# Moving the wait for the output weights from TensorE to SyncE, in a decode attention block

## Chip, cores and metric

One core of a Trainium2 chip. The metric is device time in microseconds (us) of one execution, as the median of several runs; lower is better. All runs that are compared are fast unless a run is called slow (here: over 1.5% above the fastest run of the same kernel). "Span" is the profiled time from the first to the last instruction, some 1.8 us shorter than the device time.

## The reference, cut to what matters

```python
B, Sq, D = (8, 1, 512);  Hq, Hkv, Sk, Dh = (32, 8, 8192, 128)          # bf16
mod = (_silu(c) @ w_mod).reshape(8, 6, 1, -1)                          # sa, ca, ga, sb, cb, gb
h = _layernorm(x) * (1 + ca) + sa
q = (h @ wq) ...                                                       # 32 heads, 4 to a key/value head
p = _softmax(einsum('bhqd,bhkd->bhqk', q, k) * Dh ** (-0.5))
x = x + ga * (einsum('bhqk,bhkd->bhqd', p, v) ... @ wo)                # wo: 4096 x 512
h = _layernorm(x) * (1 + cb) + sb
x = x + gb * (relu(h @ w1 + b1) ** 2 @ w2 + b2)                        # 512 -> 1792 -> 512
```

The key and value caches are 268 MB of the 284 MB that are read.

## The kernel before

Every engine has a list of operations with their dependencies; a dependency becomes a wait on a semaphore in front of the operation. TensorE, VectorE and ScalarE run a hardware loop over the 8 batches; SyncE issues all loads unrolled.

```python
# _looped: waits on what is loaded outside the loop are emitted in front of the loop
for i in range(passes):
    for p in "ab":
        for j, o in enumerate(self._part(e, (i, p))):
            want = self._want(e, o, i)
            ...
            self._emit(eng, None, {s: v for s, v in want.items() if s not in per}, seen)
with nc.Fori(0, passes, ...) as i:
    ...                                        # part "a": every pass
    with eng.If(i < passes - 1):               # part "b": every pass but the last
        ...
```

```python
RING = sb("ring", [128, NSLOT, UNIT], BF16)    # NSLOT = 4 slots of 4 MB: two heads' keys or values
units = [(kv, b, p) for b in range(B) for kv in "kv" for p in range(NP)]     # 4 key, 4 value loads a batch

def load(n):
    ...
    dep = [released.get(s)]                    # the last reader of slot n % 4
    ...                                        # (the last value load goes in four pieces)
    loaded[n] = dma("sync", s_ring[s], lambda e: e.dma_start(slot(s), src), dep)

load(0)
load(1)
...                                            # three small bias loads
d_wo = dma("sync", s_wo, ...)                  # output weights, 4 MB
load(2)
load(3)
```

```python
for b in range(B):
    for p in range(NP):                        # keys: transpose on TensorE (L488), copy out, scores (L505)
        for k in range(4):
            t, toks = key_tiles(n, k, qn % 2)
            ...
            if k == 3:
                released[n % NSLOT] = score_first[0]
                load(n + NSLOT)
    ...                                        # softmax
    for p in range(NP):                        # values (L636)
        if p == NP - 1:                        # projection of 24 of 32 heads, reads wo_sb (L543)
            proj_done = project(...)
            values(0, 16, 28)
        ...                                    # one of the four L660 matmuls releases the slot, then load(n + NSLOT)
# behind the loop: the last value load, the last projection (L731, reads wo_sb), the MLP
```

`pe_stream` and `pe_stream32` issue filler matmuls whose results nobody reads.

## Time and profile before

| | before |
|---|---|
| device time, median | 668.92 us (668.77 to 669.64, 3 runs) |
| span | 667.0 us |
| bytes read | 283.66 MB |
| DMA share of the span, SyncE's queue | 99.2% |
| TensorE busy; mean granted clock | 79%; 0.945 |
| TensorE idle before its first key transpose | 25.53 us, ended by the landing of `wo` |

The lines are in the prediction below. To read them: a group or timeline line is "start, duration, engine, source line, operation, output<-inputs, shapes, count", and the bracket behind it is the engine's idle time just before and what ended it. In the stretches, the last three columns are the granted TensorE clock, the busy share of the 16 DMA engines and GB/s.

### The profile page before, as it was taken

What the parts mean: (1) busy time and instruction counts of PE and PEld (TensorE: products, weight loads), DVE (VectorE), ACT (ScalarE), POOL (GpSimd) and SP (SyncE); (2) the same over time, 40 slices, a digit from 0 to 9 for tenths busy, and PEclk for the clock granted to TensorE, in tenths of its full rate; (3) what the DMA queues carried; (4) which work ended last, traced back from release to release, by engine and by line L of the source; (5) the groups of instructions that cost most, each with busy time, mean ns of one, the idle gap of its engine ahead of it and who ended that gap; (6) DMA issues with size and microseconds to landing.
All of it is one profiled execution on the core that took longest, in us unless ns stands there. A gap on an engine that the chain in (4) does not pass through costs nothing.

```text
span 667.0 us, 15923 instructions
## 1 busy us (share of the span) xinstructions
PE 523.9 (79%) x7259; PEld 349.1 (52%) x7259; DVE 307.6 (46%) x587; ACT 264.4 (40%) x307; POOL 20.6 (3%) x79
## 2 busy tenths in 40 slices
PE   3309988898849987699858988399875997589887
PEld 2207753675328742477327753287434773277535
DVE  1105662567216651367314663166523673156623
ACT  2105661466106651266314661156512663146611
POOL 7400000000000000000000000000000000000000
PEclk9999999999979999799987999799997999889996
DMA  9999999999999999999999999999999999999997
GB/s 374 439 409 437 431 417 437 432 426 432 438 428 426 434 440 428 424 436 436 428 426 438 428 430 432 438 428 424 436 438 430 424 436 430 430 432 436 428 418 278
DMA packets 12188, 283.85 MB, mean 426 GB/s; under 512 B 1260, under 2 KB 1296, under 8 KB 3600
## 3 DMA queue, kind: packets, MB, share of 16 engines
q1 hardware_dynamic: 12128, 283.65, 99.2%
q8 instruction: 9, 0.15, 0.1%
q10 hardware_dynamic: 48, 0.02, 0.0%
q14 instruction: 3, 0.02, 0.0%
HBM read 283.66 MB, written 0.01 MB: 425 GB/s over the span
## 4 chain that ended last, share of the span: by engine, by line
PE 54%; DMA 36%; ACT 6%; DVE 2%; issue 1%; POOL 0%; SPq 0%; POOLq 0%; DVEq 0%
PE PS L488 37%; DMA ring<-in_A_k_cache_dram 25%; PE PS L505 10%; DMA wo_sb<-in_A_wo_dram 7%; ACT P_sb L582 5%; DMA ring<-in_A_v_cache_dram 4%; PE PS L636 2%; PE PS L478 1%; ACT KTb L493 1%; DVE O_sb L656 1%; PE PS L472 1%; PE PS L594 1%; DVE Pm L608 0%; PE PS L614 0%; PE PS L773 0%
## 5 line engine op out<-in xcount | busy, mean ns | idle before, releaser
L488 PE MATMUL PS<-IDENT,ring 128*128 128x128 bf16 x4096 | 262.4, 225 | 63.1 <-DMA ring<-in_A_k_cache_dram 35.7
L488 PEld LDWEIGHTS PS<-IDENT,ring 128*128 128x128 bf16 x4096 | 241.9, 101 | 111.4 <-issue 48.1
L493 ACT ACTIVATE KTb<-PS 128x1024 bf16<-128x1024 bf16 x192 | 196.7, 1024 | 234.4 <-PE PS L488 234.4
L495 DVE COPY KTb<-PS 128x1024 bf16<-128x1024 bf16 x320 | 209.7, 687 | 149.1 <-PE PS L488 146.9
L636 PE MATMUL PS<-ring,Pm 128*32 128x512 bf16 x1018 | 66.5, 405 | 23.5 <-DMA ring<-in_A_v_cache_dram 22.7
L505 PE MATMUL PS<-KTb,Qb 128*32 128x512 bf16 x1024 | 78.8, 384 | 4.5 <-ACT KTb L493 4.5
L656 DVE CAST O_sb<-PS 128x512 bf16<-128x512 f32 x31 | 21.4, 692 | 110.3 <-PE PS L636 110.3
L636 PEld LDWEIGHTS PS<-ring,Pm 128*32 128x32 bf16 x1018 | 26.6, 101 | 60.2 <-DMA ring<-in_A_v_cache_dram 31.4
L535 ACT ACTIVATE KTb<-PS 32x192 bf16<-32x192 f32 (+1 forms) x18 | 5.6, 311 | 112.1 <-PE PS L472 105.6
L582 ACT ACTIVATE P_sb<-PS,negm 128x1024 bf16<-128x1024 f32 x32 | 35.2, 1113 | 20.2 <-DVE negm L577 20.2
L478 PE MATMUL PS<-ONES 128*128 128x512 f32 x80 | 42.1, 630 | 0.0
L472 PE MATMUL PS<-IDENT 128*128 128x512 bf16 x112 | 33.4, 380 | 0.0
L594 PE MATMUL PS<-IDENT,P_sb 128*128 128x128 bf16 x256 | 19.8, 220 | 15.4 <-ACT P_sb L582 15.4
L608 DVE COPY Pm<-PS 64x512 bf16<-64x512 bf16 x48 | 20.2, 421 | 25.1 <-PE PS L594 24.6
L594 PEld LDWEIGHTS PS<-IDENT,P_sb 128*128 128x128 bf16 x256 | 14.4, 98 | 25.2 <-ACT P_sb L582 25.2
L505 PEld LDWEIGHTS PS<-KTb,Qb 128*32 128x32 bf16 x1024 | 15.4, 94 | 21.0 <-ACT KTb L493 8.5
L512 DVE TENSOR_REDUCE m<-PS 128x1 f32<-128x512 f32 x32 | 22.0, 689 | 6.6 <-PE PS L505 6.6
L660 PEld LDWEIGHTS PS<-SEL,O_sb 128*128 128x128 bf16 x124 | 5.8, 97 | 29.4 <-DVE O_sb L656 29.4
L478 PEld LDWEIGHTS PS<-ONES 128*128 128x128 f32 x80 | 12.7, 190 | 10.6 <-issue 10.6
L660 PE MATMUL PS<-SEL,O_sb 128*128 128x8 bf16 x124 | 7.8, 169 | 12.3 <-DVE O_sb L656 12.0
L472 PEld LDWEIGHTS PS<-IDENT 128*128 128x128 bf16 x112 | 9.9, 104 | 10.1 <-issue 7.2
L543 PE MATMUL PS<-wo_sb,KTb 128*32 128x512 bf16 x192 | 11.8, 380 | 3.3 <-ACT KTb L535 3.3
(134 smaller groups left out, 150.1 us busy)
## 6 DMA issues: line engine op xcount, KB each, us to landing
ring<-in_A_k_cache_dram SPq DMA_DIRECT2D x32, 4096.0 KB, 32.1
ring<-in_A_v_cache_dram SPq DMA_DIRECT2D x31, 4096.0 KB, 27.9
ring<-in_A_wq_dram SPq DMA_DIRECT2D x1, 4096.0 KB, 20.1
wo_sb<-in_A_wo_dram SPq DMA_DIRECT2D x1, 4096.0 KB, 46.7
ring<-in_w_mod_dram SPq DMA_DIRECT2D x1, 3072.0 KB, 10.5
ring<-in_A_v_cache_dram SPq DMA_DIRECT2D x1, 2048.0 KB, 23.1
ring<-in_B_w_dram SPq DMA_DIRECT2D x3, 512.0 KB, 19.7
ring<-in_B_w_dram SPq DMA_DIRECT2D x1, 1344.0 KB, 18.5
```

The lines of the kernel that those rows point to most:

```text
L472: ts = [op("tensor", lambda e: e.matmul(bank(at).rearrange("p (a r) -> p a r", a=4), IDENT[:, :], rhs)) for _ in range(n)]
L478: ts = [op("tensor", lambda e: e.matmul(bank(at).rearrange("p (a r) -> p a r", a=4), ONES[:, :], rhs)) for _ in range(n)]
L488: t = op("tensor", lambda e, j=j, i=i: e.matmul(STG[j][:, i, :], src[:, 32 * k + 8 * j + i, :], IDENT[:, :], is_transpose=True), [loaded[n ...
L493: stg_free[j] = op("scalar", lambda e, j=j, dst=dst: e.activation(dst, STG[j], ACT.Copy), [t])
L495: stg_free[j] = op("vector", lambda e, j=j, dst=dst: e.tensor_copy(dst, STG[j]), [t])
L505: t = op("tensor", lambda e, hf=hf, q=q, rhs=rhs: e.matmul(PS[32 * q:32 * (q + 1), k, :], Qb[:, 2 * p + hf, :], rhs, start=(p == 0 and hf ...
L512: return op("vector", lambda e: e.tensor_reduce(m4[:, k:k + 1], bank(k), AX.X, ALU.max), [t])
L582: exps.append(op("scalar", lambda e, k=k: e.activation(P_sb[:, k, :, :, :], bank(k).rearrange("p (i x) -> p i x", i=8).unsqueeze(2).to_bro ...
L594: t = op("tensor", lambda e, k=k, i=i: e.matmul(STG[k][:, i, :], P_sb[:, k, i, :, :].rearrange("p h x -> p (h x)"), IDENT[:, :], is_transp ...
L608: done.append(op("vector", lambda e, dst=dst, frm=frm: e.tensor_copy(dst, frm), [t, k_pm]))
L636: t = op("tensor", lambda e, m=m, cg=cg, p=p, vt=vt, Obank=Obank: e.matmul(Obank[32 * cg:32 * (cg + 1), :], lhs[:, p, 32 * m:32 * m + 32], ...
L656: t = op("vector", lambda e, osb=osb, Obank=Obank: e.tensor_copy(osb, Obank), [t])
```

## The change

The intent: TensorE should not stand at the loop's entry for the output weights, which it first reads after the values of three pairs of heads. SyncE waits for them instead before it issues the fifth load; TensorE waits for that load before it comes to the projection, so the order still holds. The whole diff:

```diff
-            dep = [released.get(s)]
+            dep = [released.get(s), d_wo if n == NSLOT else None]
...
                         wo_sb[:, 4 * g + j, :], start=(g == 0), stop=(g == 5), tile_position=(0, 32 * j)),
-                        k_oP + [d_wo])
+                        k_oP)
```

## The prediction

> **What bounds the kernel now.** I read four views in this order: the page (engine shares, the 40 slices, the DMA queues), the chain that ended last, the timelines of TensorE and SyncE around the wait in question, and the DMA's share stretch by stretch. First the page:
>
> ```profile
> PE 523.9 (79%) x7259; PEld 349.1 (52%) x7259; DVE 307.6 (46%) x587; ACT 264.4 (40%) x307; POOL 20.6 (3%) x79
> ...
> DMA  9999999999999999999999999999999999999997
> GB/s 374 439 409 437 431 417 437 432 426 432 438 428 426 434 440 428 424 436 436 428 426 438 428 430 432 438 428 424 436 438 430 424 436 430 430 432 436 428 418 278
> ...
> q1 hardware_dynamic: 12128, 283.65, 99.2%
> ```
>
> The DMA row is at its top digit in every slice but the last. SyncE's queue q1 alone carries 283.65 MB and fills 99.2% of the time of all sixteen DMA engines. TensorE is busy 79% of the span, so it waits somewhere for a fifth of it. Now the chain of waits and the timeline of TensorE:
>
> ```profile
> 4.21 46.74 DMA wo_sb<-in_A_wo_dram
> 51.65 5.00 PE PS L488 x64
> ...
> 107.23 22.50 DMA ring<-in_A_k_cache_dram
> ```
>
> ```profile
> 25.82 0.29 PE L435 MATMUL PS<-KTb 128*128 128x32 bf16 x4 [0.48 <-ACT KTb L432]
> 51.65 5.00 PE L488 MATMUL PS<-IDENT,ring 128*128 128x128 bf16 x64 [25.53 <-DMA wo_sb<-in_A_wo_dram]
> ```
>
> The first fence (start, length, what) says that the chain runs through the 4 MB load of the output weights (`wo`) from 4.21 to 50.95 us, and then through TensorE's key transposes. The second says that TensorE does nothing for 25.53 us in front of its first key transpose and is released by that load. This is the visible prize. But the wait is not needed by the transposes: the program puts every wait of the loop on something loaded outside it in front of the loop, and the projection, which does read `wo`, starts only at 113.96 us.
>
> The question is whether TensorE's lost 25 us reach the end. The stretches (busy time of PE, PEld, DVE, ACT, POOL, then clock, DMA share, GB/s) say no:
>
> ```profile
> 27.50:51.50 24.00, 0.00 (x0) 0.00 (x0) 0.23 (x1) 0.00 (x0) 1.47 (x5) 1.00 1.00 418
> 51.50:120.00 68.50, 61.55 (x871) 41.41 (x871) 37.09 (x68) 32.19 (x37) 0.00 (x0) 1.00 1.01 431
> 120.00:640.00 520.00, 428.40 (x5956) 287.36 (x5960) 256.62 (x467) 223.38 (x256) 0.00 (x0) 0.94 1.00 432
> ```
>
> While TensorE stands still, the DMA engines are full (share 1.00, 418 GB/s), and in the two later stretches they are just as full. The idle time belongs to an engine that is not the bound.
>
> Landings confirm it. From the trace's completion records, the sixteenth completion of each 4 MB load comes at 30.92 us (key load 0), 40.66 (key 1), 50.94 (`wo`), 61.00 (key 2), 70.84 (key 3), 81.17, 90.88, 100.60, 110.31 (the four value loads) and 120.02 (the first key load of batch 1). From 120.02 on they come every 9.716 us: 54 loads later, at 644.69, (644.69 - 120.02)/54. This is 4.194 MB / 9.716 us = 432 GB/s without a pause. The end hangs on the same stream: the value chunks are all in at 654.67, and the last chunk of the second MLP weight at 663.56. The last MLP matmuls are stopped by it: the step between their starts is 0.15 us right after that landing against 0.03 us among the others. The span ends 3.4 us later, at 667.0.
>
> [...] `wo`, issued at 4.21, lands after 46.74 us just by standing behind earlier loads. [...] Key load 2's issue in the timeline of SyncE is such a one (14.98 to 37.63); the 24 us it blocks hurt nothing, because queued bytes cover them.
>
> ```profile
> 14.98 23.70 SPq L369 DMA_DIRECT2D ring<-in_A_k_cache_dram  x2
> 61.87 0.33 SPq L369 DMA_DIRECT2D ring<-in_A_v_cache_dram  x1
> ```
>
> **The change part by part.**
> 1. *TensorE's wait in front of the loop goes.* It then waits for key load 0, landed at 30.92. Between `wo`'s landing and the first transpose lay 51.65 - 50.94 = 0.7 us (loop entry); part of the entry can now be done earlier, so the first transpose comes at 31.0 to 31.6, 20 us sooner.
> 2. *TensorE in batch 0 then runs into the loads.* A key load costs it 9.76 us (four times 1.89 of transposes and 0.55 of scores), nearly the DMA's 9.7. Key 0 until 41, key 1 until 51, then it stands 10 us until key 2 lands at 61.00. Key 3 lands at 70.84, just as key 2 is done; key 3 is done by 80.6. Softmax took 10.5 us before (from 90.8 to the first value matmul at 101.33), so values start near 91; loads 2 and 3 of them land only at 100.60 and 110.31, and the last values are done near 113.5 instead of 118.2. The next key load lands at 120.02. TensorE started batch 1 at 120.08 before and will start it there again. All 20 us are given back inside batch 0: worth at the end 0.0.
> 3. *SyncE's wait comes in front of the fifth load (value 0).* Slot 0 comes free near 41.5, `wo` lands at 50.94: the issue moves from 61.87 to about 51.0. At 51.0 the queue still holds key 2 and 3, until 70.84, i.e. 19.8 us of work. Before, at 61.87, it held 70.84 - 61.87 = 9.0 us. So the margin grows, but it was never used up: cost 0.0, gain 0.0.
> 4. *Ordering.* TensorE needs `wo` only after value loads, which SyncE issues after its wait. So nothing is added in the loop. The projection of the last two heads (L731) lies behind the loop and keeps its wait; as TensorE no longer waits in front of the loop, the wait is now actually emitted: about 0.05 us (TensorE's waits show 51 ns in the trace) on the final chain, partly behind the last MLP weights. I count 0 to +0.1.
>
> Sum: -0.0 - 0.0 + 0.05, on 668.92.
>
> **The rivals.**
> *(a) TensorE's head start is kept*: 51.65 - 31.5 = 20 us off, 648.8, 3.0% faster. For it: the chain, which charges 7.0% to the `wo` load, and TensorE's 79%. Against it: no DMA pause anywhere into which the loads could move forward; [...] after batch 0 TensorE waits again (the 22.50 us piece above is the stream, seen from TensorE).
> *(b) The stream is a little looser early on, and deeper queueing tightens it.* Slices 3 and 6 show 409 and 417 GB/s, and between `wo` and value 0 the spread from the first to the last engine's completion grows from 1.2 to 2.3 us and stays. If an earlier issue cured that, about -1.1 us, 667.8. Against it: the engine completing first keeps its 9.7 us step throughout, and the growth falls together with 16 KB instruction fetches (nine in the trace, near 1.1 us each, seven of them from 55 to 111). These have to come anyway, only sooner.
> *(c) SyncE's wait starves the queue.* It would take `wo` landing later than 70.8; slowed by early fetches it might land a microsecond later, not 20. If it did occur, some us slower, 670 to 675.
> *(d) SyncE's issue becomes slow because more is queued.* Issues later in this trace with 25.9 us of work ahead take the same 0.33 us. 0.0.
>
> **Range and chances.** The three runs before lie from 668.77 to 669.64. I take 668.8, with -1.0 for (b) and +1.0 for the spread of runs and point 4. Two percent is 13.4 us: only (a) comes near on the one side and a starved queue on the other, and both contradict the DMA row, so 2% for faster and 1% for slower.
>
> **What would show it.** In the changed profile: the first key transpose near 31.5 us; the value 0 issue near 51 and value 1 right behind it; a wait of SyncE on `wo` of about 12 us; a TensorE gap of some 10 us before key load 2 and others among the values; the first key transpose of batch 1 at 120 us as before; landings and the last MLP weight's landing within 1 us of before; DMA share 99%. The prediction is wrong if TensorE's batch 1 starts well before 120, if any slice shows DMA under 9, or if the steady step between landings differs from 9.72 us.

"Such a one", in front of SyncE's timeline, means an issue that takes long; the one named took 22.6 us (14.98 to 37.63), with the DMA share at 0.98 and 421 GB/s meanwhile. 0.0, 0.0 and 0.05 on 668.92 come to 668.97, and I took 668.8, in 667.8 to 669.8. For loads already issued, the trace of the changed kernel shows: while SyncE waited (38.60 to 51.31 us), they went on at a DMA share of 1.01 and 408 GB/s.

## The result, and the profile after

| | before | after |
|---|---|---|
| device time, median | 668.85 us (668.68 to 669.64, 4 runs) | 668.37 us (668.15 to 668.45, 4 runs) |
| ratio, 95% interval | | 0.999 (0.9973 to 1.0007) |
| span | 667.0 us | 666.7 us |
| first key transpose | 51.65 us | 30.84 us |
| value load 0 issued | 61.87 us | 51.38 us |
| first key transpose of batch 1 | 120.08 us | 119.86 us |
| last MLP weight landed | 663.56 us | 663.33 us |
| mean granted TensorE clock | 0.945 | 0.918 |

A ratio compares means of runs of the same rounds and, in the experiments below, leaves out the profiled run of each kernel, so it is not quite the ratio of the medians. The 0.5 us between the medians did not come back in two repeats (below).

The page of the changed kernel, same lines as in the prediction:

```profile
PE 528.3 (79%) x7259; PEld 352.2 (53%) x7259; DVE 307.9 (46%) x587; ACT 264.3 (40%) x307; POOL 20.5 (3%) x79
...
DMA  9999999999999999999999999999999999999997
...
q1 hardware_dynamic: 12128, 283.65, 99.3%
```

The DMA row is the same in every slice; TensorE's share too. The clock in the table needs care. In the trace of the kernel before, the clock's records begin only at 54.33 us, and all time before counts as full clock, also the stretch from 27.50 to 51.50 us in which TensorE did nothing. That the clock was not full at the end of it is read from the first 64 transposes: 5.00 us at 51.65, against 3.73 us at 120.08, where the record is at full. The changed kernel's records begin at 14.5 us and hold 34 us of half clock before 124 us; from there on the two traces have 73 and 75 us of it. 34 us at half clock are 0.026 of the span, nearly the whole step from 0.945 to 0.918. Of these 34 us, 13.7 lie before 54.33 us, where the trace of the kernel before has no records, and 20.5 behind it, where its records are at full. How much of the step is only where the records begin, the two traces do not show.

The timeline of TensorE in the changed kernel shows where the 20 us went:

```profile
30.84 5.71 PE L488 MATMUL PS<-IDENT,ring 128*128 128x128 bf16 x64 [5.11 <-DMA ring<-in_A_k_cache_dram]
...
61.61 3.60 PE L488 MATMUL PS<-IDENT,ring 128*128 128x128 bf16 x32 [9.89 <-DMA ring<-in_A_k_cache_dram]
65.14 0.87 PE L505 MATMUL PS<-KTb,Qb 128*32 128x512 bf16 x8
65.94 1.96 PE L488 MATMUL PS<-IDENT,ring 128*128 128x128 bf16 x32
...
110.15 3.54 PE L636 MATMUL PS<-ring,Pm 128*32 128x512 bf16 x32 [2.97 <-DMA ring<-in_A_v_cache_dram]
114.49 0.26 PE L660 MATMUL PS<-SEL,O_sb 128*128 128x8 bf16 x4 [0.81 <-DVE O_sb L656]
119.86 5.57 PE L488 MATMUL PS<-IDENT,ring 128*128 128x128 bf16 x64 [5.12 <-DMA ring<-in_A_k_cache_dram]
```

TensorE starts when key load 0 lands (30.79 us) and then waits for loads: 9.89 us for key load 2, 2.97 us for value load 3, 5.12 us for the first key load of batch 1. After the last of these it stands where it stood before; the same view of the kernel before has there

```profile
115.25 1.91 PE L636 MATMUL PS<-ring,Pm 128*32 128x512 bf16 x32
117.96 0.26 PE L660 MATMUL PS<-SEL,O_sb 128*128 128x8 bf16 x4 [0.80 <-DVE O_sb L656]
120.08 3.73 PE L488 MATMUL PS<-IDENT,ring 128*128 128x128 bf16 x64 [1.86 <-PEq L151]
```

(PEq is TensorE's sequencer, L151 the loop's turn; the key load landed at 120.02 there.) So 3.5 us of lead were left at the end of batch 0 (114.49 for 117.96), and the key load that lands at 119.82 takes them away. SyncE's waits in the changed kernel (engine, line, releaser: us in total, times, longest) and its timeline:

```profile
SPq L116 <- DMA wo_sb<-in_A_wo_dram: 12.7, 1, 12.7
```

```profile
51.38 31.83 SPq L369 DMA_DIRECT2D ring<-in_A_v_cache_dram  x4
```

SyncE waits 12.7 us for the weights, and then issues value loads 0 and 1 at 51.38 and 51.75, with 19.6 and 28.5 us of earlier loads still to land by the trace's completion records. Before, value load 0 had 8.6 us ahead of it when it had been issued. The tightest place before was the first key load of batch 1, with 5.7 us; in the changed kernel it has 13.8 us. The change gave slack, not time. The stretches after (columns as in the prediction) match those of before, DMA share 1.00 and 416, 430, 432 GB/s:

```profile
27.50:51.50 24.00, 20.66 (x312) 17.11 (x312) 13.29 (x21) 11.55 (x12) 1.46 (x4) 0.86 1.00 416
51.50:120.00 68.50, 45.49 (x566) 26.83 (x562) 24.23 (x49) 20.61 (x26) 0.00 (x0) 0.88 1.00 430
120.00:640.00 520.00, 429.26 (x5952) 289.14 (x5951) 256.49 (x466) 223.24 (x256) 0.00 (x0) 0.93 1.00 432
```

TensorE's 20.66 us of work in the first stretch was missing in the second: 45.49 for 61.55.

### The profile page after: what moved, and what is told of

Read it like the earlier page. It is cut to its first block, busy times and chain, and to the rows that moved or that the text cites. A ratio compares the mean times of both kernels' runs of the same rounds, so it can differ in the third digit from the quotient of the medians.

```text
span 666.7 us, 15924 instructions
## 1 busy us (share of the span) xinstructions
PE 528.3 (79%) x7259; PEld 352.2 (53%) x7259; DVE 307.9 (46%) x587; ACT 264.3 (40%) x307; POOL 20.5 (3%) x79
## 3 DMA queue, kind: packets, MB, share of 16 engines
q1 hardware_dynamic: 12128, 283.65, 99.3%
## 4 chain that ended last, share of the span: by engine, by line
PE 52%; DMA 38%; ACT 6%; DVE 2%; issue 1%; SPq 0%; DVEq 0%
PE PS L488 36%; DMA ring<-in_A_k_cache_dram 33%; PE PS L505 9%; ACT P_sb L582 5%; DMA ring<-in_A_v_cache_dram 4%; DMA ring<-in_A_wq_dram 2%; PE PS L636 2%; PE PS L478 1%; ACT KTb L493 1%; DVE O_sb L656 1%; PE PS L472 1%; PE PS L594 1%; DVE Pm L608 0%; PE PS L614 0%; PE PS L773 0%
## 5 line engine op out<-in xcount | busy, mean ns | idle before, releaser
L488 PE MATMUL PS<-IDENT,ring 128*128 128x128 bf16 x4096 | 267.1, 227 | 56.2 <-DMA ring<-in_A_k_cache_dram 56.2
L488 PEld LDWEIGHTS PS<-IDENT,ring 128*128 128x128 bf16 x4096 | 246.5, 102 | 104.8 <-DMA ring<-in_A_k_cache_dram 57.4
L535 ACT ACTIVATE KTb<-PS 32x192 bf16<-32x192 f32 (+1 forms) x18 | 5.6, 310 | 110.0 <-PE PS L472 103.9
L478 PEld LDWEIGHTS PS<-ONES 128*128 128x128 f32 x80 | 12.7, 190 | 10.6 <-issue 10.6
## 6 DMA issues: line engine op xcount, KB each, us to landing
ring<-in_A_wq_dram SPq DMA_DIRECT2D x1, 4096.0 KB, 19.8
```

The lines of the kernel that those rows point to most:

```text
L478: ts = [op("tensor", lambda e: e.matmul(bank(at).rearrange("p (a r) -> p a r", a=4), ONES[:, :], rhs)) for _ in range(n)]
L488: t = op("tensor", lambda e, j=j, i=i: e.matmul(STG[j][:, i, :], src[:, 32 * k + 8 * j + i, :], IDENT[:, :], is_transpose=True), [loaded[n ...
```

## The experiments

The theories: **stream theory**, the queue of loads sets the end and TensorE's start has slack; **clock theory**, TensorE sets the end, and a granted clock that fell by 2.9% (0.945 to 0.918) ate a gain of 3%, 20 us; **SyncE theory**, SyncE's new wait costs what TensorE's start gains. All edits are to the changed kernel.

### The changed kernel again (two runs)

No edit.

> The changed kernel once more, unedited, to see whether its 0.5 us below the kernel before are there on another run. Stream theory (the queue of loads sets the end, TensorE's start does not): 668.2 to 668.9, ratio 0.998 to 1.000. Clock theory (TensorE sets the end, and the lower granted clock, 0.918 for 0.945, ate a gain of 20 us): the same time, so this run does not tell them apart, but the clock should again be near 0.918.

> The changed kernel in the same rounds, as partner of the run with SyncE's wait two loads later. Stream theory: 668.2 to 668.9, ratio to the kernel before 0.9985 to 1.0010.

Measured: 668.62 us (668.23 to 669.92), ratio 1.0004 (0.9991 to 1.0016); and 668.42 us (668.29 to 669.84), ratio 1.0002 (0.9989 to 1.0015). The 0.5 us of the first comparison are within the scatter. The clock again is 0.915 to 0.918 in the profiled runs. But the kernel *before* in these rounds, unedited, had clocks between 0.912 and 0.947, with 668.37 us at 0.919 and 668.19 at 0.947: the clock figure differs from run to run and the time does not follow. That the start of the records makes this difference is likely, but not shown: no trace of these runs is kept. In these rounds the kernel before, the changed one and the next two versions all have single runs at 669.5 to 670.3; what makes these is open.

### TensorE's wait put back, SyncE's kept

```diff
         qn = 0
         norm_last = None
+        Pg.wait("tensor", [d_wo])
```

> SyncE's wait stays, TensorE's wait on the output weights in front of the loop is put back. Stream theory: first key transpose back at 51.7 us, value load 0 issued near 62, and the time that of the kernel before, 668.6 to 669.2; batch 1 starts at 120.0 as ever. Rival 'SyncE's wait costs what TensorE's start gains': the cost of SyncE's wait would now stand alone, so some us above the kernel before, 672 or more. Clock theory: 668.9 with the clock back at 0.945.

Measured: 668.65 us (668.33 to 670.15), ratio 1.0003 (0.9991 to 1.0015). TensorE starts at 51.54 us and value load 0 is issued at 62.90. With both waits and with SyncE's alone (668.62) the time is the same, so TensorE's earlier start, and the earlier issue that comes with it, are worth nothing. On the cost of SyncE's wait the run says nothing, against what I expected of it: here the weights are in (50.95 us) before the slot of value load 0 comes free, so the wait holds nothing up. The next experiment tests it. The clock did not go back to 0.945 (0.921), against what the clock theory needed; but the records begin at 15.6 us here, so this figure compares with the changed kernel's and not with 0.945.

### SyncE's wait two loads later (two runs)

```diff
-            dep = [released.get(s), d_wo if n == NSLOT else None]
+            dep = [released.get(s), d_wo if n == NSLOT + 2 else None]
```

> SyncE waits for the output weights two loads later, in front of the seventh, where they have long landed, so that the wait holds up nothing. Stream theory: value load 0 is issued near 41.5 us instead of 51.4 and value load 1 near 51.5, landings and time unchanged, 668.2 to 668.7. Rival 'SyncE's wait costs': faster by what it cost, up to 10 us, 658 to 667.

> SyncE's wait two loads later, repeated, because four of its five runs lay 1 us above the rest. If that is chance (the kernel before has single runs at 669.5 to 670.3 too): median 668.3 to 669.0 and a ratio within 0.001 of the changed kernel's in the same rounds. If the earlier issue really costs: again 669.5 or more and a ratio of 1.0015 or more.

Measured: first 669.68 us, ratio 1.0016 (1.0003 to 1.0029), above the expected range; repeated 668.65 us, ratio 1.0005 (0.9993 to 1.0018), against 1.0002 of the changed kernel in the same rounds. Value load 0 is issued at 42.24 and 42.45 us. Nine microseconds of earlier issue bring nothing, so SyncE's wait, which held the issue up by that much, cost nothing. The first run's 1 us did not repeat; I count it as the scatter above.

### Half of the output weights

```diff
-            wo_sb[:, :, :].rearrange(...),
-            A_wo.rearrange("(g p j) n -> p g (j n)", g=8, p=128)))
+            wo_sb[:, 0:16, :].rearrange(...),
+            A_wo[0:2048].rearrange("(g p j) n -> p g (j n)", g=4, p=128)))
...                                             # both readers: wo_sb[:, (4 * g + j) % 16, ...]
```

> Half of the output weights is loaded (2 MB instead of 4) and used twice; wrong result on purpose. Nothing of TensorE's work changes. Stream theory: 2.097 MB fewer at 432 GB/s, so every later landing and the end come 4.9 us earlier: 663.0 to 664.2. Clock theory (TensorE sets the end): no change, 668 to 669.

Measured: 663.41 us (663.17 to 663.55), ratio 0.9921 (0.9906 to 0.9935): 5.1 us less than the kernel before in the same rounds, for 4.9 expected. The queue line of its page:

```profile
q1 hardware_dynamic: 11616, 281.56, 99.3%
```

The share stays at 99.3% while 2.1 MB fewer pass. The last MLP weight lands at 657.94 us, 5.4 us before that of the changed kernel. Fewer bytes move the end; 20 us of TensorE's start did not.

### TensorE's start delayed further (two runs)

```diff
         qn = 0
         norm_last = None
+        Pg.op("tensor", lambda e: e.wait_ge(s_ring[2], 16))     # key load 2; the other run: s_ring[3], key load 3
```

> TensorE starts its key transposes only when key load 2 has landed (61.5 us), 10 us later than in the kernel before and 31 later than in the changed one. Stream theory: value load 0 is issued near 72.3 and finds the queue just empty (key load 3 in at 71.3), and the first key load of batch 1 is issued near 114.7, when the fourth value load is already in (113); about 3 us and 3.6 us of stream are lost: 673 to 677. If TensorE's start passed straight to the end: 668.9 + 10.4 = 679 against the kernel before. If the start did not matter at all: 668.5.

> The same with key load 3 (71.3 us), another 10 us later. Stream theory: value load 0 is issued near 82, the queue has then been empty for 11 us,[...] and the first key load of batch 1 lands near 136 instead of 119.8: 682 to 687, so of the step from the run with key load 2 nearly all 10 us reach the end. If TensorE's start passed straight to the end: 689.

The second expectation: 673 to 677 of the first, and nearly all of the 10 us of later start, come to 682 to 687. The 3 and 3.6 us of the first are my estimates.

Measured: 676.43 us (676.14 to 677.5), ratio 1.0115 (1.0097 to 1.0133); and 687.12 us (686.56 to 687.87), ratio 1.027 (1.0252 to 1.0288), 0.1 us above the expected range. The profiles say how. SyncE's timeline and the stretches with key load 2:

```profile
71.67 29.59 SPq L369 DMA_DIRECT2D ring<-in_A_v_cache_dram  x4
114.05 14.24 SPq L369 DMA_DIRECT2D ring<-in_A_k_cache_dram  x4
```

```profile
60.00:80.00 20.00, 18.87 (x288) 15.73 (x289) 11.88 (x18) 10.47 (x11) 0.00 (x0) 1.00 0.83 343
80.00:120.00 40.00, 36.40 (x504) 23.16 (x505) 22.62 (x43) 19.79 (x24) 0.00 (x0) 1.00 0.96 395
120.00:640.00 520.00, 428.93 (x5980) 289.12 (x5972) 256.38 (x466) 222.78 (x254) 0.00 (x0) 0.94 1.00 432
```

Key load 3 lands at 70.65 us, value load 0 is issued at 71.67 and its first packet starts 0.96 us later, and the DMA share falls to 0.83 and 0.96. Against 432 GB/s the stretches lose 20 x (1 - 343/432) + 40 x (1 - 395/432) = 4.1 + 3.4 = 7.5 us, and the time is 676.43 - 668.47 = 8.0 us longer. The stream had been expected to lose 6.6; TensorE's own delay is 61.13 - 51.65 = 9.5. With the second dose, from 61.13 to 71.16, 10.7 us more of time come out of 10.0 us more of delay. So TensorE's start counts fully only after the point where SyncE finds the queue empty. Starts at 30.84, 51.54, 61.13 and 71.16 us gave 668.6, 668.65, 676.4 and 687.1 us.

### More work for TensorE (four runs)

In every batch, 12 fillers in front of the values:

```diff
-            pe_stream(2, 1)
+            pe_stream(14, 1)
```

> Twelve more filler matmuls of TensorE in each of the 8 batches, in front of the first value matmul, about 0.22 us apart, so some 2.6 us a batch and 21 us in all. Stream theory: the loads have at least 13.6 us queued whenever one is issued, so 2.6 us fit into TensorE's waits and nothing comes at the end: 668.0 to 669.2. Clock theory (TensorE sets the end): +21 us, 689.

Measured: 669.92 us (669.54 to 670.34), ratio 1.0011 (0.9995 to 1.0028). It is not the 21 us of the clock theory, yet its four runs lie above the range that I had given, and the profiled span is 1.9 us longer. The timeline of TensorE in the last batch, first with the fillers, then of the changed kernel:

```profile
639.75 1.91 PE L636 MATMUL PS<-ring,Pm 128*32 128x512 bf16 x32
...
655.10 0.82 PE L636 MATMUL PS<-ring,Pm 128*32 128x512 bf16 x10
```

```profile
637.09 1.91 PE L636 MATMUL PS<-ring,Pm 128*32 128x512 bf16 x32
...
652.52 0.82 PE L636 MATMUL PS<-ring,Pm 128*32 128x512 bf16 x10
```

The 2.6 us of the last batch are still there at 655 us: from the last batch's key transposes on, TensorE no longer waits for a load long enough to hide them (its list of waits in the changed kernel has no DMA from 615 us on). The last MLP matmuls (L773) then start 2.3 us later (663.97 for 661.68), and 0.4 us are regained there, because they no longer wait for the last weight: it landed at 663.20, as early as in the changed kernel, so the 1.9 us are TensorE's and not the stream's. In the last batch, TensorE's own work and the stream end together. The other seven batches' fillers, some 18 us, left no trace. So I moved the fillers into the part of the loop that the last pass skips:

```diff
                     elif p == NP - 2:
                         pe_stream(1, 4)
+                    elif p == NP - 1:
+                        pe_stream(24, 4)      # then pe_stream32(10, 4), then pe_stream32(6, 4)
```

> 24 filler matmuls of TensorE (about 0.22 us apart, 5.2 us) behind the last value load's matmuls in each of the first 7 batches, none in the last: 36 us in all. Stream theory, as mended after the run with fillers in every batch (only the last batch's TensorE work has no slack): nothing at the end, 668.2 to 669.7. Clock theory, or TensorE as the bound throughout: +36 us, near 705. If the mend is wrong and the loss there came from every batch a little: about +2 us, 670.5 or more.

> The same test with the same time but fewer instructions: 10 filler matmuls in fp32 (0.53 us apart, 5.3 us) in each of the first 7 batches, 37 us in all, instead of 24 in bf16, whose run fetched 45 instruction packets instead of 9 and stood at the loop's turn for up to 8.9 us. If that refetching was the cause of its 686: 9 or 10 instruction packets here and, by the stream theory, 668.2 to 669.7. If TensorE's extra time was the cause: again 680 or more with 9 packets.

> 6 fp32 fillers instead of 10 in each of the first 7 batches. An fp32 filler takes 1.06 us of TensorE (10.94 us for ten in the trace of the run before), so 6.4 us a batch, 45 us in all; they add 24 instructions to a pass of the loop, as the run with fillers in every batch did (1783 a pass, 9 instruction packets), instead of 40 (1799 a pass, 18 packets). Stream theory, if refetching was what hurt: 9 packets, no long loop turn, 668.2 to 669.9. If TensorE's time hurts by itself: 675 or more. TensorE as the bound throughout: +45 us, 713.

Measured: with 24 bf16 fillers three fast runs at 680.96, 685.01 and 687.14 and a slow one at 691.44, against the expectation. With 10 fp32 fillers two fast runs at 671.0 and 672.56 and two slow ones at 681.15 and 684.83: also missed. (Ten took 10.94 us in the first batch, twice what was planned.) The ratios, 1.0284 and 1.0122, reckon the 691.44 and the 681.15 in; the fast runs alone lie 2.3% and 0.5% above the kernel before. With 6 fp32 fillers 669.27 us (668.43 to 669.71), ratio 1.0011 (0.9995 to 1.0028): as expected. The line of the instruction queue on the page, in this order:

```profile
q8 instruction: 45, 0.74, 0.5%
```

```profile
q8 instruction: 18, 0.29, 0.2%
```

```profile
q8 instruction: 9, 0.15, 0.1%
```

The kernels before and after have 9. The traces have 1759 TensorE records in a pass of the changed kernel's loop, 1783 in the passes with 12 bf16 or 6 fp32 fillers, 1799 with 10 fp32 and 1807 with 24 bf16 fillers. The first three kernels fetch their loop once (9 packets; in the changed kernel's trace seven from 34.3 to 102.9 us, in the first pass, and two behind the loop, at 654.7 and 662.3); the last two fetch it again (18 and 45 packets). TensorE's waits in the 24-filler kernel:

```profile
PE PS L488 <- issue: 32.8, 5, 8.9
```

That is idle time at the loop's turn, up to 8.9 us, in which the branch itself shows as 5.9 to 7.5 us long in the trace, four times, where 0.2 us is usual. The step from 1783 to 1799 records with the packets is shown. It is not that every pass of the longer loop fetches: the 24-filler trace has three passes without a packet (none from 191 to 437 us), the 10-filler trace six (none from 194 to 657). What sets the fetching off, and why these turns take so long, is open. The runs with refetching say nothing on the theories. The clean one does: the fillers of the last kernel take 5.40 us a batch in its trace, 38 us in all:

```profile
114.56 5.40 PE L478 MATMUL PS<-ONES 128*128 128x512 f32 x12
```

TensorE's busy time goes from 528.3 to 557.6 us:

```profile
PE 557.6 (84%) x7343; PEld 355.7 (53%) x7343; DVE 307.6 (46%) x587; ACT 264.3 (40%) x307; POOL 20.5 (3%) x79
```

Its span is that of the changed kernel, 666.7 us. TensorE is not the bound before the last batch; the clock theory falls.

No version in these runs beats both kernels, other than the one with half of the weights, whose result is wrong.

## Why the prediction was right

**The sum.** Predicted 668.8 us in 667.8 to 669.8; measured 668.37, and 668.62 and 668.42 in the repeats. "Worth at the end 0.0" is what the runs show: the end follows bytes (half of the weights, -5.1 us), not TensorE's start. The signs that the prediction named hold too: from 119.82 to 644.46 us the landings still come every 9.716 us, and the DMA row is at 9 in every slice but the last, which was at 7 before as well.

**Step 1, TensorE's wait goes.** First transpose predicted at 31.0 to 31.6, measured 30.84, a little earlier, 0.05 us after the landing of key load 0: the loop entry is wholly done before.

**Step 2, the lead is given back inside batch 0.** Right, with one term too small. The 10 us gap before key load 2 is there (9.89). I had not counted that TensorE came out of it slow: the first 32 transposes took 3.60 us instead of 1.96. The trace's clock record is at half from 55.46 to 65.70 us, with TensorE idle from 51.72 to 61.61. Key load 2 also landed 0.56 us later than assumed (61.56). Both together made the values start at 93.08 us instead of 91. The last ones were done at 114.75 instead of 113.5 for a reason of their own: the 32 matmuls after the gap of 2.97 us took 3.54 us instead of 1.91, at half clock again (110.08 to 113.49). The key load at 119.82 hid all this. The 64 transposes behind that load, after 5.12 us idle, took 5.57 us instead of 3.73; the record goes from half to full at 123.73, when only transposes had run since 119.86.

**Step 3, SyncE's wait.** Predicted issue at 51.0 with 19.8 us of work queued; measured 51.38 with 19.6 left when the issue was done. The run with the wait two loads later shows that it cost nothing; the run with both waits, issued at 62.90, shows that the earlier issue gained nothing. One reading was off, without effect: the issue of key load 2 took 22.6 us, not 24; why it took so long, no run tests.

**Step 4, the wait behind the loop.** The wait is emitted, but the predicted 0.05 us are not there: in the changed trace one wait instruction in front of the last projection waits for `wo` and for ScalarE's copies (L535) together, where the kernel before has one for the copies alone. The projection starts 0.09 us after the last copy (L537), before the change 0.16 us; at the end nothing of it can be told from the scatter.

**The rivals.** (a) fell by the trace and by the clean filler run: the 7.0% of the span that the chain charged to the load of the output weights were worth 0.0. (b), a tighter stream by 1.1 us: the spread between first and last engine still comes to 2.2 us, and the repeats have ratios 1.0004 and 1.0002; not seen. (c) did not occur; of (d) there is a trace: value load 1 took 0.77 us to issue instead of 0.33, with 28.5 us queued, without effect.

**What the prediction left out.** It said that the end hangs on the stream. That is half of it: in the last batch TensorE's chain has no slack either, as the fillers in every batch showed with their 1.9 us of span. Had the change lengthened TensorE's last batch, it would have been slower.

## What to carry to other kernels

An idle time on one engine is worth something only if the engine or queue that is full can use it (here TensorE started 20.8 us sooner beside a queue at 99.2%, for 0.0): look for a pause on the full one first, and for the place where the lead will be caught up. Such a change still moves slack (5.7 to 13.8 us here), which shows only when something else gets later; measure slack by delaying on purpose, in two doses, and look at the last pass of a loop by itself. When instructions are added as a probe, count the instruction fetches, since a loop that fetches again measures something else (here 18 and 45 packets for 9, with idle times at its turn of up to 8.0 and 8.9 us).
